# One step list for attention and router: 213 of 471 steps elsewhere, 20 entries of the engine tables changed

## The chip, the cores and the metric

The kernel runs on one core of a Trainium2 chip. Engines: TensorE for matmuls (PE; its weight loads are shown as PEld), VectorE (DVE), ScalarE (ACT), GpSimd (POOL) and SyncE (SP), which issues nearly all transfers (DMAs). The metric is the device time of one execution in microseconds. Three runs of the kernel before took 601.49, 602.51 and 603.44 us; the median is 602.51 us. A further execution was profiled: 600.41 us, of which 598.3 us lie between its first and its last instruction (the span). Times inside a trace are counted from the start of the span.

## The reference, cut to what matters

Three blocks follow one another on 2 x 768 tokens of 512 numbers:

```python
# attention, 2 batches x 8 heads x 768 x 64: local window of 16, plus one key and value per block of 32
k_sum = k.reshape(B, H, nb, 32, D).max(axis=3); v_sum = v.reshape(B, H, nb, 32, D).mean(axis=3)
a = softmax(concat([masked scores q.k, scores q.k_sum + log 32]))
x = a @ concat([v, v_sum])                      # then heads side by side: 1536 x 512
# router and experts: each token to the expert with the largest logit
logits = x/|x| @ (emb/|emb|).T / tau;  expert = argmax(logits);  gate = softmax(logits)[expert]
y[mask] = gate * (relu(x[mask] @ w1[e]) @ w2[e])    # 8 experts, 512 -> 1024 -> 512
# rational feed-forward, 512 -> 2048 -> 512
h = y @ w_in;  g = P(h) / (Q(h) + 1e-6);  out = g @ w_out
```

All is in float32; the large matrices go through the matmul engine as a high and a low part (whi and wlo, xhi and xlo).

## The kernel before, in words

The change touches the first part alone: attention, the router and the start of the experts. After it come 17 expert slots of 128 tokens (gemm1 at L967, gemm2 at L998) and the feed-forward (L946 to L948 and L1327), both unchanged.

Every engine runs its own instructions in the order in which the program emits them; there is no scheduler behind it (`manual_schedule`). SP's transfers are such a queue too. So the order in which Python calls the functions below is the order on each engine.

Attention works on 8 head pairs (n = 0 to 7; 0 to 3 are batch 0) and on 24 groups (g) of four blocks of 64 queries. Groups 0 to 2 read pair 0, 3 to 5 pair 1, 6 to 11 pairs 2 and 3, 12 and 13 pair 4, 14 and 15 pair 5, 16 to 19 pairs 6 and 7, 20 to 23 pairs 4 to 7. Tokens come in 12 chunks (c) of 128 for the router, which takes them two by two (k = 0 to 5). I name the steps by the letters that the new list uses:

- L n loads k, q and v of a pair (L147 to L158), W n the two halves of its windowed values vp (L160). Pair 0 and most of pair 1 are loaded ahead. The buffers of q and k are three, those of bd, kw and vw five.
- K n (prep_k, L171) builds the block-diagonal queries bd in two halves, the block maxima ks, their broadcast copy into kw, and the window copy into kw (I write bd5, ks7, kwb7 for the broadcast, kw7 for the window). The table BDE names the engines of the halves, KE that of the window copy: A is ACT, D is DVE, P is POOL.
- V n (prep_v, L199) sums values by blocks, on DVE or as a tree of six adds on POOL (VE). P n (prep2, L214) transposes the sums on PE and copies them to vw on ACT.
- S g scores on PE (L266), N g row minima on DVE (L280), X g exponentials on ACT (L288), T g transposes on PE (L294) and a copy on ACT or DVE (AE), O g the product with the values (L316), E g three DVE operations that divide and write the chunk (L323, L325, L331).
- f c transposes a chunk on PE (L390) and copies it (XE), q c its squares (QE; on POOL a tree of ten), Z c the logits (L423), m c maximum and its place on DVE, w c writes the chunk to memory; h, d, u, p k make the one-hot (L448), the ranks on PE (L498 to L505), the running sum (L453) and the two one-hot matrices (L522, L524). I 0 to I 4 set the router up, I 5 to I 7 load the first expert weights (w1(0), w2(0), w1(1)).
- The end: n0 to n2 norms, PC counts, tb the table of slots on DVE, F1 to F5 the tokens of the slots, g0 and g1 gathers on POOL, x0 the first slot's transposes, i and j the high parts of the first weights on ACT, l the low parts (wlo, L691), z0, z1, rc, rg the gates, k and y matmuls that only keep PE busy.

In the kernel before, the order comes from two places. For groups 0 to 22 a loop (L636) emits S g, T g-2, E g-4, N g, X g, O g-3, and then what the tables GK, GV, G2, GL, GR, GW, FO, FX and FQ put at that group, each function as a whole. From E19 on, the string DRAIN (L65) lists the steps one by one, and a step of several operations is advanced by one each time that it is named.

The scores' buffers in PSUM are two (ps_s), so S g needs N g-2 done; the transposes' buffer is one (ps_t), so a T needs the copy of the T before.

## Time and profile before

| | |
|---|---|
| runs | 601.49, 602.51, 603.44 us |
| profiled execution | 600.41 us, span 598.3 us |
| mean clock of PE | 0.986 of 2.4 GHz |
| PE busy | 573.0 us (96% of the span) |
| DVE busy | 471.4 us (79%) |
| ACT busy | 418.6 us (70%) |
| POOL busy | 264.0 us (44%) |
| first S | 6.62 us |
| first gemm1 matmul (L967) | 101.79 us |
| DMA share in the first ten of 40 slices, in tenths | 8 9 9 9 8 1 3 6 6 8 |

A slice is 15 us. The first seven slices are attention and router; in them the digits of PE are 4 8 9 8 9 9 9 and those of DVE 5 9 9 9 8 8 9. The waits name who released an engine that sat idle; an engine can be the limit of one stage and be idle in the next, so the shares over the whole span say little of these seven slices.

### The profile page before, as it was taken

The page shows a single profiled execution, that of the slowest core. Times are in us where ns is not written, and L with a number is a line of the kernel's source. Part 1 is how long each engine was busy: PE and PEld are TensorE (multiplying, and loading weights), DVE is VectorE, ACT ScalarE, POOL GpSimd, SP SyncE. Part 2 cuts the span into 40 slices and gives each one's busy share as a digit, 9 for nine tenths or more (in the row PEclk, how much of TensorE's full clock was granted, in tenths as well). Part 3 has the DMA queues.
Part 4 walks back from the last instruction along what each step waited for, and adds up shares of the span by engine and source line. Part 5 has one row for each costly group of instructions (what it writes and reads, how often), then busy time and mean ns, then how long its engine had stood idle before and what let it go on. Part 6 is the DMA issues. An engine that isn't in the chain of part 4 may idle for free. (4 is left out here: it accounts for less than half of the span.)

```text
span 598.3 us, 10282 instructions
## 1 busy us (share of the span) xinstructions
PE 573.0 (96%) x3137; PEld 468.3 (78%) x3137; DVE 471.4 (79%) x1025; ACT 418.6 (70%) x716; POOL 264.0 (44%) x281
## 2 busy tenths in 40 slices
PE   4898999999999999999999999999999999999994
PEld 3787885788888888888887888888888888888883
DVE  5999888978844896769777888888997777778874
ACT  5998845774536564566866998777778887766762
POOL 6478161158333550634032664414445763423424
PEclk9998997999999999999999999999999999999998
DMA  8999813668669996789974323110324200100101
GB/s 296 322 308 304 336 71 108 199 242 280 215 230 294 379 317 194 253 313 341 354 249 132 118 73 122 54 53 1 109 86 158 71 1 1 53 19 0 54 18 70
DMA packets 38749, 101.65 MB, mean 170 GB/s; under 512 B 6105, under 2 KB 6233, under 8 KB 38690
## 3 DMA queue, kind: packets, MB, share of 16 engines
q1 hardware_dynamic: 36210, 92.81, 46.1%
q0 software_dynamic: 2480, 8.15, 4.3%
q8 instruction: 25, 0.41, 0.3%
q14 instruction: 34, 0.28, 0.1%
HBM read 119.51 MB, written 19.18 MB: 232 GB/s over the span
## 5 line engine op out<-in xcount | busy, mean ns | idle before, releaser
L926 POOL TENSOR_SCALAR el<-el 128x512 f32<-128x512 f32 x32 | 66.9, 2098 | 95.0 <-ACT el L921 94.9
L691 DVE TENSOR_TENSOR wlo<-rw,whi 128x1024 fp32r<-128x1024 f32 x64 | 77.6, 1272 | 0.9 <-ACT whi L688 0.4
L1127 POOL TENSOR_TENSOR wlo<-el,whi 128x512 fp32r<-128x512 f32 (+1 forms) x33 | 42.2, 1278 | 77.2 <-ACT whi L1126 37.3
L688 ACT ACTIVATE whi<-rw 128x1024 fp32r<-128x1024 f32 x64 | 63.9, 1053 | 9.2 <-DMA rw<-w 3.7
L998 PE MATMUL py<-whi,hhi 128*128 128x512 f32 x136 | 53.9, 404 | 0.2 <-ACT hhi L985 0.2
L998 PE MATMUL py<-whi,hlo 128*128 128x512 f32 x136 | 52.7, 396 | 0.0
L967 PE MATMUL ph<-whi,xhi 128*128 128x512 f32 x128 | 49.8, 407 | 0.3 <-ACT xhi L681 0.3
L967 PE MATMUL ph<-whi,xlo 128*128 128x512 f32 x128 | 48.7, 397 | 0.0
L986 DVE TENSOR_TENSOR hlo<-pht,hhi 128x512 fp32r<-128x512 f32 x34 | 21.8, 682 | 27.9 <-ACT hhi L985 27.8
L1113 ACT ACTIVATE el<-el 128x512 f32<-128x512 f32 (+1 forms) x49 | 30.6, 624 | 14.9 <-DVE el L1107 14.8
L1327 PE MATMUL acc<-whi 128*128 128x512 f32 x130 | 39.1, 394 | 0.7 <-ACT whi L1126 0.7
L1105 ACT ACTIVATE el<-hg,ab 128x512 f32<-128x512 f32 (+1 forms) x33 | 22.4, 680 | 24.4 <-PE hg L948 24.3
L946 PE MATMUL hg<-x2h,whi 128*128 128x512 f32 (+1 forms) x100 | 39.5, 395 | 0.0
L947 PE MATMUL hg<-x2h,wlo 128*128 128x512 f32 (+1 forms) x100 | 39.2, 392 | 0.0
L948 PE MATMUL hg<-x2l,whi 128*128 128x512 f32 (+1 forms) x100 | 39.1, 391 | 0.0
L1327 PE MATMUL acc<-whi,wlo 128*128 128x512 f32 x130 | 38.7, 391 | 0.4 <-POOL wlo L1127 0.4
L1327 PE MATMUL acc<-wlo,whi 128*128 128x512 f32 x130 | 38.5, 390 | 0.0
L1119 DVE SCALAR_TENSOR_TENSOR el<-el,ab,hg 128x512 f32<-128x512 f32 (+1 forms) x33 | 24.3, 738 | 16.0 <-ACT hg L1115 15.2
L1127 POOL TENSOR_TENSOR xlo<-el,xhi 128x512 fp32r<-128x512 f32 (+1 forms) x16 | 20.2, 1262 | 37.6 <-issue 21.1
L1107 DVE SCALAR_TENSOR_TENSOR el<-el,ab,hg 128x512 f32<-128x512 f32 (+1 forms) x33 | 24.4, 738 | 15.4 <-ACT el L1106 15.2
L1114 ACT ACTIVATE el<-el,ab 128x512 f32<-128x512 f32 (+1 forms) x49 | 35.1, 717 | 1.6
L998 PE MATMUL py<-wlo,hhi 128*128 128x512 f32 x136 | 34.4, 395 | 0.0
(584 smaller groups left out, 1615.4 us busy)
## 6 DMA issues: line engine op xcount, KB each, us to landing
...
```

The costliest lines, as they stand in the source:

```text
L688: nc.scalar.activation(out=whi[:, i], in_=rw[s % 2, i // 4][:, i % 4], func=AF.Copy)
L691: eng.tensor_tensor(out=wlo[:, i], in0=rw[s % 2, i // 4][:, i % 4], in1=whi[:, i].bitcast(F32), op=ALU.subtract)
L926: eng.tensor_scalar(out=z, in0=z, scalar1=CLO, scalar2=CHI, op0=ALU.max, op1=ALU.min)
L946: nc.tensor.matmul(out=o, lhsT=lh, rhs=rh, start=start, stop=False)
L947: nc.tensor.matmul(out=o, lhsT=ll, rhs=rh, start=False, stop=False)
L948: nc.tensor.matmul(out=o, lhsT=lh, rhs=rl, start=False, stop=stop)
L967: nc.tensor.matmul(out=ph[n], lhsT=l[:, k], rhs=w, start=(k == 0 and not rl and l is hi), stop=(k == 3 and rl))
L998: nc.tensor.matmul(out=py, lhsT=l[:, f], rhs=w, start=(f == 0 and not rl and l is hi), stop=(f == 7 and rl))
L1113: nc.scalar.activation(out=a, in_=a, func=AF.Abs)
L1114: nc.scalar.activation(out=r, in_=a, func=AF.Ln, bias=ab[:, 7:8])
L1127: nc.gpsimd.tensor_tensor(out=lo, in0=g, in1=hi.bitcast(F32), op=ALU.subtract)
L1327: nc.tensor.matmul(out=acc[q], lhsT=l[:, q * P - o:(q + 1) * P - o], rhs=r, start=start, stop=stop)
```

## The change

The loop, its tables and DRAIN go; one string SCHED lists all 471 steps, and the generators get more yields, so that K, L, W can be taken apart too. Both lists hold the same steps; in the longest common order stand 258, the other 213 are at another place. Twenty entries of the tables BDE, VE, KE, QE, AE, XE and SE name another engine.

```diff
--- before.py
+++ after.py
@@ -41,31 +41,32 @@
 NTOK = B * S
 NT = NTOK // P
 E = 8
-BDE = {0: 'AA', 1: 'PD', 2: 'AA', 3: 'PD', 4: 'DA', 5: 'PD', 6: 'DP', 7: 'AA'}
-VE = {0: 'D', 1: 'P', 2: 'P', 3: 'D', 4: 'P', 5: 'P', 6: 'P', 7: 'P'}
-GK = {1: 1, 2: 3, 3: 4, 4: 9, 5: 11, 6: 11, 7: 13}
-GV = {1: 3, 2: 4, 3: 6, 4: 10, 5: 11, 6: 12, 7: 13}
-G2 = {0: 1, 1: 3, 2: 6, 3: 7, 4: 11, 5: 13, 6: 15, 7: 17}
-GL = {2: 0, 3: 0, 4: 5, 5: 7, 6: 7, 7: 11}
-QE = "PDDDADADPPDA"
-GR = [1, 5, 5, 8, 9, 12, 20, 19]
-GW = {1: 1, 2: 1, 3: 6, 4: 3, 5: 9, 6: 17, 7: 18}
-AE = "DADAAAAAAAAADAAAAAAAADAD"
-XE = "DADAADADAAAA"
-KE = {0: 'A', 1: 'D', 2: 'D', 3: 'A', 4: 'A', 5: 'P', 6: 'A', 7: 'P'}
-FO = [10, 11, 13, 15, 16, 18, 20, 21, 22, 23]
-FX = [4, 11, 15, 20, 14, 19, 22, 21]
-FQ = [15, 16, 15, 22, 17, 18, 18, 18, 22]
+BDE = {0: 'AA', 1: 'PA', 2: 'AA', 3: 'PD', 4: 'DA', 5: 'PP', 6: 'DD', 7: 'AA'}
+VE = {0: 'D', 1: 'P', 2: 'P', 3: 'P', 4: 'P', 5: 'P', 6: 'P', 7: 'P'}
+QE = "APDPAPADPDPA"
+AE = "AADAAAAAAAAADAAAAAAAADAA"
+XE = "AADDAAAADAAA"
+KE = {0: 'D', 1: 'D', 2: 'D', 3: 'A', 4: 'P', 5: 'P', 6: 'A', 7: 'P'}
 STOP = False
-MICRO = True
-TRACE = []
-SE = "DDDD"
+SE = "DPDD"
 NX, NM = 22, 26
 TS, OS = (), (0, 2)
-DRAIN = ("E4 T2 h3 E4 S E4 w8 w9 O3 M O2 T1 Z8 O1 d3 X m8 E3 E3 m8 E3 f9 E2 E2 E2 T0 f10 Z9 E1 u3 p3 p3 p3 u3 u3 R0 "
-         "E1 m9 E1 p3 O0 m9 Z10 R1 E0 E0 h4 d4 E0 w10 w11 u4 m10 f11 p4 Z11 p4 m10 q10 q9 p4 C p4 q11 n0 n1 u4 m11 u4 n2 n2 "
-         "i0 m11 h5 d5 n2 p5 PC k2a tb p5 n2 tb p5 n2 p5 F1 tb F2 g0 i2 tb n2 tb F3 k4b i1 tb tb tb tb tb i3 tb K0 k3a tb tb "
-         "K1 k1a tb K2 k1b tb j0 j1 F4 F5 g1 tb x0 k2b z0 z1 rc l0 rg l1 l2 l3 ")
+SCHED = ("K0 K0 K0 K0 K0 K0 K0 K0 V0 L3 S0 N0 X0 L2 L2 P0 S1 N1 L2 L3 S2 K1 K1 K1 K1 X1 K1 W1 L3 W1 I0 N2 T0 S3 "
+         "X2 T1 V1 P1 N3 K2 K2 K2 K2 K2 X3 W4 O0 S4 E0 E0 N4 X4 K3 T2 V2 E0 S5 K3 K3 K3 W2 W2 L4 K3 T3 I1 O2 N5 "
+         "X5 L5 O1 E1 E1 E1 I2 W3 W3 S6 T4 O3 E2 W4 L4 L4 E2 E2 V3 P2 S7 O4 L5 L5 N6 X6 T5 E3 S8 N7 X7 E3 I3 T6 "
+         "E4 E4 E4 P3 N8 X8 E3 O5 W5 E5 E5 E5 S9 T7 N9 O6 X9 K4 K4 K4 K4 K4 L6 L6 E6 E6 V4 I4 T8 E6 K5 S10 N10 "
+         "X10 O7 f0 S11 P4 T9 E7 E7 E7 N11 X11 L7 L6 L7 L7 w1 O8 K5 K5 Z0 K5 K5 E8 f1 K6 K6 m0 w0 V5 S12 N12 O9 "
+         "T10 K6 K7 E8 Z1 S13 m1 K7 m1 V6 T11 m0 h0 I5 E8 K6 E9 X12 E9 E9 K6 O10 P5 N13 X13 K7 S14 f2 N14 X14 T12 "
+         "O11 d0 S15 p0 E10 V7 K7 K7 E10 E10 f3 w2 u0 u0 u0 Z2 m2 m2 N15 T13 O12 E12 W6 X15 q2 P6 E11 S17 E12 E12 "
+         "q1 E11 E11 W5 S16 N16 p0 p0 Z3 T14 p0 f4 X16 O13 E13 E13 T15 N17 O14 m3 m3 w4 P7 S18 T16 w5 Z4 h1 E14 "
+         "E14 W6 E14 N18 X18 W7 q4 O15 E13 E15 E15 I7 f5 W7 m4 S19 T18 X17 m4 E15 q5 d1 p1 O16 N19 E16 u1 S20 T17 "
+         "u1 u1 X19 p1 p1 Z5 N20 E16 E16 O17 f6 E17 X20 m5 m5 h2 I6 E17 E17 S21 N21 p1 T19 q3 X21 S22 O18 Z6 q7 "
+         "m6 d2 f7 w7 p2 u2 u2 T20 E18 E18 E18 u2 N22 O19 q6 p2 f8 p2 p2 Z7 m7 q0 m7 q8 m6 h3 w3 w6 T21 S23 N23 "
+         "E19 E19 E19 q9 O20 X22 T22 Z8 O22 X23 O21 E20 E20 m8 m8 f9 E21 E21 E21 d3 p3 T23 Z9 E20 u3 f10 E22 E22 "
+         "p3 u3 p3 p3 E22 O23 Z10 w8 m9 m9 E23 E23 h4 u3 E23 w11 d4 w10 u4 f11 m10 m10 p4 p4 q10 Z11 C w9 p4 p4 "
+         "q11 n0 n1 u4 m11 m11 h5 d5 k2a n2 n2 n2 n2 p5 i0 p5 n2 p5 p5 PC tb tb n2 F1 tb tb j1 j0 F2 g0 u4 k4b tb "
+         "tb tb tb tb tb tb y0 tb tb tb tb i2 k3a i1 F3 y1 k1a i3 y2 k1b F4 F5 tb g1 x0 l0 l1 z0 z1 rc rg l2 l3 "
+         "k2b ")
 NEG = 1.0e30
 RS = 1536
 NA = E * RS // P
@@ -148,6 +149,7 @@
         b, hp = slots[n]
         q_t, k_t = qks[n % 3][:, 0:S], qks[n % 3][:, S:QK]
         nc.sync.dma_start(out=k_t, in_=I["kT"][b, hp, :, 0:SP])
+        yield
         nc.sync.dma_start(out=q_t, in_=I["qT"][b, hp])
         raw[n] = (q_t, k_t)
 
@@ -161,6 +163,8 @@
         b, hp = slots[n]
         i = n % NS
         for c in range(2):
+            if c:
+                yield
             j = slice(c * NJ // 2, (c + 1) * NJ // 2)
             nc.sync.dma_start(out=vw[i][LOC:LOC + WLP, j].rearrange("p j d -> p (j d)"),
                               in_=I["vp"][b, hp, c, :, 0:NJ * DV])
@@ -183,11 +187,14 @@
                 else:
                     nc.gpsimd.tensor_tensor(out=bd[i][s, j0:j1, s], in0=src,
                                             in1=eighth[s].unsqueeze(2).to_broadcast([64, NJ, QB]), op=ALU.mult)
+                yield
             if j0 == 0:
                 ks = wk.tile([P, NB], F32, name="ks")
                 nc.vector.tensor_reduce(out=ks, in_=k_t[:, WIN - 1:WIN - 1 + S].rearrange("p (n r) -> p n r", r=32),
                                         axis=AX.X, op=ALU.max)
+                yield
                 nc.vector.tensor_copy(out=kw[i][:, :, 0:NB], in_=ks.unsqueeze(1).to_broadcast([P, NJ, NB]))
+                yield
             if KE[n] == "D":
                 nc.vector.tensor_copy(out=kw[i][:, j0:j1, LOC:KW], in_=win(k_t, j0, j1))
             elif KE[n] == "A":
@@ -195,6 +202,7 @@
             else:
                 nc.gpsimd.tensor_tensor(out=kw[i][:, j0:j1, LOC:KW], in0=win(k_t, j0, j1),
                                         in1=one.unsqueeze(2).to_broadcast([P, j1 - j0, WL]), op=ALU.mult)
+            yield
 
     def prep_v(n):
         v_t = raw.pop(n)[2]
@@ -226,13 +234,16 @@
     ab = const.tile([P, 8], F32, name="ab")
     vcs = {}
     zero(0, nc.vector)
-    load_qk(0)
+    for _ in load_qk(0):
+        pass
     mask = cload("mask", [P, 3, KW])
     load_v(0)
     cst = cload("cst", [P, NCST])
     ident = cst[:, 0:P]
-    load_qk(1)
-    load_w(0)
+    for _ in load_qk(1):
+        pass
+    for _ in load_w(0):
+        pass
     load_v(1)
     nc.sync.dma_start(out=emb, in_=I["emb"])
     nc.sync.dma_start(out=tau, in_=I["tau"].to_broadcast([E, 1]))
@@ -566,21 +577,9 @@
     def keep_pace(src):
         nc.tensor.matmul(out=env["warm"][0:1, 0, 0:E], lhsT=src[:, 0:1], rhs=src[:, 0:E], start=True, stop=True)
 
-    prep_k(0)
-    prep_v(0)
-    LT, LO, LE = 2, 3, 4
-    sched = {}
     bts = {}
     xTs = {}
     zs_ = {}
-
-    def at(g, fn, *args):
-        sched.setdefault(g, []).append((fn, args))
-
-    def f1_(c, q=True):
-        xTs[c] = router_a(c)
-        if q:
-            router_q(c)
 
     def fz_(c):
         zs_[c] = router_z(c, xTs.pop(c))
@@ -592,55 +591,13 @@
                 bts[i] = dict(c0=2 * i, n=2, **{x: b6[x][:, 2 * i:2 * i + 2] for x in ("z", "m8", "i8")})
         return router_m(c, zs_.pop(c), bts[k])
 
-    def f2_(k, c):
-        fz_(c)
-        lace(fm_(k, c))
+    def fa_(c):
+        xTs[c] = router_a(c)
 
     def loads(n):
-        load_qk(n)
+        yield from load_qk(n)
+        yield
         load_v(n)
-
-    for n in range(8):
-        if n:
-            at(GK[n], prep_k, n)
-            at(GV[n], prep_v, n)
-        at(G2[n], prep2, n)
-    for n, g in GW.items():
-        at(g, load_w, n)
-    for n, g in GL.items():
-        at(g, loads, n)
-    for g, fn in zip(GR, (router_init0, router_init1, router_init4, router_init3, router_init2,
-                          lambda: wload(0, 0), lambda: wload(0, 1), lambda: wload(1, 0))):
-        at(g, fn)
-    batches = {0: (0, 1), 1: (2, 3), 2: (4, 5), 3: (6, 7), 4: (8, 9), 5: (10, 11)}
-    first = dict(enumerate(FO))
-    for c in first:
-        if c < 8:
-            at((max(FX[c], first[c]), 0), xw, c)
-        if c < 9:
-            at((first[c], 0), f1_, c, False)
-            at((max(FQ[c], first[c]), 0), router_q, c)
-    for k in range(4):
-        cs = batches[k]
-        for c in cs:
-            at(first[c] + 1, f2_, k, c)
-        l = first[cs[-1]]
-        for d, fn in ((2, router_h), (3, router_d), (3, router_u), (4, router_p)):
-            if k < 3:
-                at(l + d, lambda fn, k: lace(*filter(None, (fn(bts[k]),))), fn, k)
-
-    def run(g):
-        for fn, args in sched.pop(g, ()):
-            fn(*args)
-
-    for g in range(NG - 1):
-        s_mm(g)
-        t_mm(g - LT) if g >= LT else None
-        lace(o_ev(g - LE)) if g >= LE else None
-        s_sm(g)
-        o_mm(g - LO) if g >= LO else None
-        run((g, 0))
-        run(g)
 
     idx = const.tile([P, MAXS], U32, name="idx")
     xg = {}
@@ -808,68 +765,39 @@
         nc.tensor.matmul(out=pi[:, 0:MAXS], lhsT=env["mT"], rhs=sel, start=True, stop=True)
         nc.vector.tensor_scalar(out=idx[:, 1:MAXS], in0=pi[:, 1:MAXS], scalar1=float(NTOK), scalar2=None, op0=ALU.add)
 
-    G = NG - 1
-    ops = {"S": lambda: s_mm(G), "M": lambda: s_min(G), "X": lambda: s_exp(G), "C": close_att, "PC": count,
-           "tb": table, "F1": slot0_mm, "F2": slot0_ix, "F3": slots_mm, "F4": slots_ix, "F5": slots_id, "g0": lambda: gather(0), "g1": lambda: gather(1),
-           "x0": lambda: xtr(0), "gw": gw,
-           "R0": lambda: run(G), "R1": lambda: run(G + 1),
+    ops = {"C": close_att, "PC": count, "tb": table, "F1": slot0_mm, "F2": slot0_ix, "F3": slots_mm, "F4": slots_ix,
+           "F5": slots_id, "g0": lambda: gather(0), "g1": lambda: gather(1), "x0": lambda: xtr(0),
            "z0": lambda: router_z0(bts[6]), "z1": lambda: router_z1(bts[6]),
            "n0": lambda: router_n0(bts[6]), "n1": lambda: router_n1(bts[6]), "n2": lambda: router_n2(bts[6]),
            "rc": lambda: router_c(bts[6]), "rg": lambda: router_g(bts[6])}
-    for k in range(3):
-        ops[f"T{k}"] = lambda k=k: t_mm(G - k)
-    for k in range(4):
-        ops[f"O{k}"] = lambda k=k: o_mm(G - k)
-        ops[f"i{k}"] = lambda k=k: shi(0, k)
-        ops[f"l{k}"] = lambda k=k: slo(0, k, nc.gpsimd if SE[k] == "P" else nc.vector)
-    for t in DRAIN.split():
+
+    def family(name, keys, fn):
+        for k in keys:
+            ops[f"{name}{k}"] = lambda k=k: fn(k)
+
+    for name, fn in (("S", s_mm), ("N", s_min), ("X", s_exp), ("T", t_mm), ("O", o_mm), ("E", o_ev)):
+        family(name, range(NG), fn)
+    for name, fn in (("K", prep_k), ("V", prep_v), ("P", prep2), ("W", load_w), ("L", loads)):
+        family(name, range(len(slots)), fn)
+    for name, fn in (("f", fa_), ("q", router_q), ("w", xw), ("Z", fz_), ("m", lambda c: fm_(c // 2, c))):
+        family(name, range(NT), fn)
+    for name, fn in (("h", router_h), ("d", router_d), ("u", router_u), ("p", router_p)):
+        family(name, range(6), lambda k, fn=fn: fn(bts[k]))
+    family("I", range(8), lambda k: (router_init0, router_init1, router_init4, router_init3, router_init2,
+                                     lambda: wload(0, 0), lambda: wload(0, 1), lambda: wload(1, 0))[k]())
+    family("i", range(4), lambda k: shi(0, k))
+    family("j", range(4), lambda k: shi(0, 4 + k))
+    family("l", range(4), lambda k: slo(0, k, nc.gpsimd if SE[k] == "P" else nc.vector))
+    family("y", range(3), lambda k: keep_pace(env[("cs", "ge", "pr")[k]]))
+    started = {}
+    for t in SCHED.split():
         if t[0] == "k":
-            ops[t] = lambda n=int(t[1]): keep_busy(n)
-    for k, name in enumerate(("cs", "ge", "pr")):
-        ops[f"K{k}"] = lambda name=name: keep_pace(env[name])
-    for k in range(4):
-        ops[f"j{k}"] = lambda k=k: shi(0, 4 + k)
-    for k in range(5):
-        ops[f"E{k}"] = lambda k=k: o_ev(G - k)
-    for c in range(8, 12):
-        ops[f"Z{c}"] = lambda c=c: fz_(c)
-        ops[f"m{c}"] = lambda c=c: fm_(c // 2, c)
-        ops[f"w{c}"] = lambda c=c: xw(c)
-        if c > 8:
-            ops[f"f{c}"] = lambda c=c: f1_(c, False)
-            ops[f"q{c}"] = lambda c=c: router_q(c)
-    for k in range(3, 6):
-        ops[f"h{k}"] = lambda k=k: router_h(bts[k])
-        ops[f"d{k}"] = lambda k=k: router_d(bts[k])
-        ops[f"u{k}"] = lambda k=k: router_u(bts[k])
-        ops[f"p{k}"] = lambda k=k: router_p(bts[k])
-    started = {}
-    TRACE.clear()
-
-    def step(t):
+            keep_busy(int(t[1]))
+            continue
         if t not in started:
             started[t] = ops[t]()
-        g = started[t]
-        if g is None:
-            TRACE.append(t)
-            return False
-        r = next(g, 0)
-        if r is None or t not in done_:
-            TRACE.append(t)
-        if r is not None:
-            done_.add(t)
-        return r is None
-
-    done_ = set()
-    for grp in DRAIN.split():
-        ts = grp.split("+")
-        if MICRO:
-            for t in ts:
-                step(t)
-        else:
-            while ts:
-                ts = [t for t in ts if step(t)]
-    assert not sched, sched
+        if started[t] is not None:
+            next(started[t], None)
     tab_.close()
     rt_.close()
 
```

## Rows read from the trace of the kernel before

**Rows 1.** Windows by stage: start:end length, busy per engine (instructions), clock, DMA share, GB/s
```profile
20.00:50.00 30.00, 26.40 (x334) 23.09 (x329) 28.81 (x146) 29.30 (x66) 17.63 (x23) 1.00 1.03 317
58.00:80.00 22.00, 22.00 (x269) 20.01 (x267) 18.81 (x124) 16.79 (x49) 5.95 (x11) 1.00 0.73 267
80.00:102.00 22.00, 19.63 (x182) 13.60 (x177) 17.98 (x115) 11.65 (x24) 8.32 (x20) 0.84 0.30 97
102.00:116.00 14.00, 13.24 (x61) 10.03 (x61) 13.80 (x19) 8.46 (x12) 2.21 (x2) 1.00 0.53 140
```

**Rows 2.** Waits of PE, 5 to 105 us: total us, times, longest
```profile
PE pz L503 <- DVE oh L448: 2.0, 1, 2.0
```

**Rows 3.** Timeline of DVE, 47.5 to 51.5 us: start, duration, instruction
```profile
47.86 0.94 DVE L188 TENSOR_REDUCE ks<-rw 128x24 f32<-128x768 f32 x1
48.84 1.12 DVE L190 COPY kw<-ks 128x288 f32<-128x288 f32 x1
49.87 0.97 DVE L448 TENSOR_TENSOR oh<-cst,i 128x16 bf16<-128x16 f32 x1
50.77 0.68 DVE L299 COPY aT<-pt 118x512 f32<-118x512 f32 x1
```

**Rows 4.** Windows around the stretches in which PE's clock was low
```profile
48.60:52.00 3.40, 1.40 (x17) 1.30 (x14) 3.30 (x7) 2.32 (x3) 3.19 (x4) 0.99 0.97 382
52.00:55.40 3.40, 3.40 (x28) 3.06 (x28) 3.26 (x24) 2.09 (x7) 3.06 (x7) 0.51 0.78 194
89.50:96.30 6.80, 6.80 (x45) 4.55 (x46) 4.65 (x36) 3.17 (x7) 0.00 (x0) 0.50 0.56 171
```

**Rows 5.** Timeline 32 to 38 us: idle time ahead and releaser in brackets
```profile
32.22 1.06 POOL L207 TENSOR_TENSOR vs<-el 128x384 f32<-128x384 f32 x1 [10.23 <-DMA el<-vT]
...
33.86 0.54 DVE L182 TENSOR_SCALAR el<-rw 64x768 f32<-64x768 f32 x1
...
36.26 1.46 POOL L184 TENSOR_TENSOR bd<-qk,eighth 64x768 f32<-64x768 f32 x1 [0.96 <-DMA qk<-qT]
```

**Rows 6.** Durations by source line: ns min/median/max, first and last start
```profile
L190 DVE COPY kw<-ks x6: 311/542/1116, 4.9 to 48.8; 128x288 f32<-128x288 f32 x6
L448 DVE TENSOR_TENSOR oh<-cst,i x6: 145/174/967, 49.9 to 92.0; 128x16 bf16<-128x16 f32 x6
L417 DVE CUSTOM_DVE_ANT_0 junk<-xall x6: 669/684/785, 55.6 to 88.8; 128x512 bf16<-128x512 f32 x6
L691 DVE TENSOR_TENSOR wlo<-rw,whi x64: 1162/1219/1648, 103.1 to 317.3; 128x1024 fp32r<-128x1024 f32 x64
L926 POOL TENSOR_SCALAR el<-el x32: 1906/1920/2898, 127.7 to 439.6; 128x512 f32<-128x512 f32 x32
```

**Rows 7.** Timeline 40 to 57 us: values of pair 6, kw7, exponentials, group 16
```profile
44.97 1.00 POOL L207 TENSOR_TENSOR vs<-rw 128x384 f32<-128x384 f32 x1
...
47.72 2.07 POOL L196 TENSOR_TENSOR kw<-rw,one 128x1128 f32<-128x1128 f32 x1
...
52.41 1.24 ACT L288 ACTIVATE at<-sm,nm 128x118 f32<-128x118 f32 x4 [1.48 <-DVE nm L280]
...
56.13 1.05 PE L266 MATMUL sp<-kw,bd 128*128 128x118 f32 x8
```

**Rows 8.** The page's costliest groups: POOL's splits
```profile
L1127 POOL TENSOR_TENSOR wlo<-el,whi 128x512 fp32r<-128x512 f32 (+1 forms) x33 | 42.2, 1278 | 77.2 <-ACT whi L1126 37.3
```

**Rows 9.** Timeline of ACT in the opening
```profile
14.41 0.20 ACT L355 ACTIVATE ab<-ab 128x2 f32<-128x2 f32 x1 [0.78 <-DMA ab<-ab]
```

**Rows 10.** Timeline of the tail: group 23, the first expert's matmuls
```profile
78.64 1.05 PE L266 MATMUL sp<-kw,bd 128*128 128x118 f32 x8
...
80.83 0.27 DVE L280 CUSTOM_DVE_ANT_0 sm<-sp,mask 128x118 f32<-128x118 f32 x1
...
101.79 2.13 PE L967 MATMUL ph<-whi,xhi 128*128 128x512 f32 x8 [0.25 <-ACT xhi L681]
...
108.39 0.73 PE L967 MATMUL ph<-wlo,xhi 128*128 128x512 f32 x2 [0.40 <-DVE wlo L691]
```

## The prediction

> **What bounds the kernel now.** I first read the windows of the span by stage [rows 1]. From 116 us on the matmul engine (PE) is busy in every slice of the page and the chain that ended last runs through it up to the drain at the end, so this change can only move the moment at which that stretch begins, plus what it leaves behind on VectorE (DVE) up to 116 us. In 20 to 50 us ScalarE (ACT, 29.30 of 30.00) and DVE (28.81) are both full and PE is not (26.40); in 58 to 80 us PE is full (22.00 of 22.00) and the others are not; in 80 to 102 us no engine is full and PE's clock is down (0.84); in 102 to 116 us DVE is full again (13.80 of 14.00). So four stages, each with its own limit, and an edit is priced in the stage where it lands.
>
> Then the waits of PE up to 105 us [rows 2]: the longest behind the start and the opening is 2.0 us, the rank matmul of the first pair of chunks (d0) waiting for the one-hot that DVE makes (h0). The timeline of DVE there [rows 3] shows why: the broadcast copy of ks7 takes 1.12 us and h0 0.97 us, both far above their usual size, while GpSimd (POOL) runs its own copies. The windows by clock [rows 4] show what followed: PE, idle for most of 48.6 to 52.0, got 0.51 of its clock (1.2 of 2.4 GHz) in 52.0 to 55.4; the same happened in 89.5 to 96.3.
>
> Last I read the transfers. SyncE (SP) issues the loads in order and they land in order; the reader that waits shows when: v of pair 4 releases POOL at 32.22, q of pair 5 at 36.26 [rows 5]. In the old list v4 is the 15th transfer behind v1 and q5 the 19th, hence 4.04 us for 4 places, 1.01 us a place.
>
> **The change part by part.** Counted step by step, 258 of the 471 steps keep their order among each other, 213 stand elsewhere, none is added or dropped. The tables put 20 entries on another engine; what that does to the sums of 0 to 116 us:
> - DVE loses bd1 and bd5 halves and takes one of bd6 (net one of 0.54 [rows 5]); it loses the sum of v3 (about 0.95, the size of the ks reduction beside it [rows 3]), three squares net (0.68 each [rows 6]), three transposed copies net (about 0.68, [rows 3] has one), one wlo split (1.22 [rows 6]); it takes kw0 (estimate 0.7, under the 0.94 of the reduction over the same tile). Sum: -0.54 - 0.95 - 2.04 - 2.04 - 1.22 + 0.7 = -6.1 us.
> - ACT stays within 1 us: it loses two window copies and gains copies and one square.
> - POOL gains the sum of v3 (2.75) and kw4 (2.07; both [rows 7]), two squares net (trees of ten small adds each) and wlo1. Its splits in the trace are half as wide and take 1.28 [rows 8], so 2.56 us.
>
> The opening gains nothing: kw0 on DVE lets the first scores start some tenths earlier, but ACT then waits for the small ab load in any case, until 14.41 [rows 9], and that load keeps its place.
>
> The loads. K, Q and V of pair 4 go behind the second halves of the vp tiles: q4 from place 14 to 17, so at 36.26 - 2 x 1.01 = 34.2 us, v4 from 15 to 18 (35.2), q5 stays at 19. DVE took q4 at 33.86 without a wait [rows 5]; now it waits about 0.35 us, and group 10 starts no earlier than before. What was gained ahead of it is lost here. The vp halves of pairs 5 to 7 now queue on SP behind chunk writes 4 and 5, which wait for E11; readers of W7 come four groups later, so I price this at nothing; without that cover it would be two places, 2 us.
>
> POOL's chain then runs from v4: V4 2.75 (from 44.97 to 47.72 in [rows 7]), two bd5 halves at 1.46, kw5 2.07, V5, V6, V7 2.75 each, and only then kw7 2.07: 35.2 + 2.75 + 2.92 + 2.07 + 8.25 + 2.07 = 53.3 us. Groups 16 and 17 need kw7; group 16 started at 56.13 [rows 7]. So POOL allows 2.8 us at most there.
>
> The stall at 48.6: h0 is now issued before group 13, so PE's 2.0 us wait goes and, with it, the reason for the slow clock after it. What is late next? ACT had 1.48 us of idle ahead of group 14's exponentials [rows 7]; gone, ACT allows 1.5 to 2. DVE has the same operations between the row minima of groups 13 and 15 in either list (kwb7, the copies and E10 are only shuffled past group 14), so it wins only what the two stretched operations cost, 0.81 and 0.80 (against 0.31 and 0.17 for the same lines in [rows 6]), less the 0.35 of q4: 1.2 us. The least of the three is DVE's, and I take **1.2 us** at group 16 (bounds: -4 if kw7 is late, rival A; +2.8).
>
> From 58 to 80 us PE is the limit and its work is the same, so the 1.2 us are carried, and DVE's lighter load (the squares, the copies) is hidden behind PE; if PE were not full, it would be worth up to 4 us.
>
> The tail. Group 23's minima started at 80.83 [rows 10], 2.2 us behind its first matmul, because E19 and a copy stood ahead on DVE; now E19 stands behind it. But PE puts Z8, two O and f9 between, so only part of that reaches the last chunk. And PE was busy all of 89.5 to 96.3 at half clock [rows 4], so whatever of it is not waiting could be half as long. Between 0 and 2.2, I take **0.6 us**, nearer to the end at which PE's order decides.
>
> The wlo1 split on POOL takes 1.22 us from the full DVE between 102 and 108 us; PE waited 0.40 us for the last of these splits at 108.39 [rows 10]. Between -1.3 (DVE held up for POOL's 2.56 in place of its own 1.22) and +1.2, I take **0.6 us**, nearer to the wait that PE shows.
>
> Do moved operations slow DVE? Here a row speaks: wlo on DVE takes 1.16 to 1.65 us and POOL's clip 1.91 to 2.90 [rows 6], the long ones where both run. That is about 0.4 us on DVE and 1.0 on POOL for a meeting, not the whole length of the other's instruction; it is why I leave the sums above as they are. The Trainium skill (SBUF — State Buffer, section "SBUF: two separate sides") says more: GpSimd and DVE share a port pair as an exclusive lock for the whole instruction and "the other fully blocks", for DVE operations with two SBUF inputs too. By that rule the moved wlo1 relieves nobody (rival D); the 1.65 against 1.22 agrees with a loss, not with its size.
>
> Sum: 1.2 + 0.6 + 0.6 = **2.4 us**. The profiled execution took 600.41 us (span 598.3), hence 598.0; the median of the runs shown is 602.51, 2.1 above it, hence **600.1 us**.
>
> **The rivals.**
> - A, POOL becomes the bound (slower). Place: kw7, last in POOL's chain from v4. Price: if each of the eight operations of 1 us and more in it meets DVE and takes 0.9 us longer (the 2.90 against 1.91 of [rows 6]), kw7 ends at 60.5 us; groups 16 and 17 then start 4.4 us later than in [rows 7], less 0.9 for Z2 that is already done, plus 1.7 for a slow clock behind the gap, less 1.2 of tail and wlo1: +4.0, 606.5 us. It decides from a kw7 later than about 57.3. For it: pair 4's v comes later and V3, kw4, a bd5 half stand ahead. Against it: the rows of V6 and kw7 were taken beside a full DVE and are not stretched.
> - B, the gain does not reach PE. DVE is as full between groups 13 and 15 as before and the stretched operations are stretched again, now beside kw7 at another place; only part of the tail and of wlo1 is left: -1.0, 601.5 us. For it: 28.81 of 30.00 on DVE; against it: the stall of d0 is surely gone.
> - D, wlo1 holds DVE up. POOL's 2.56 us stand in the way of the splits of rows 0, 2 and 3 on DVE, so the last one, and PE behind it, is 1.3 us later instead of 0.6 earlier: 1.2 + 0.6 - 1.3 = 0.5, hence 602.0 us. For it: the stretched rows of [rows 6]; against it: they are stretched by a third, not by the other's length. This is where the rule of the Trainium skill above would lead.
> - C, all three allowances come: 2.8 us at group 16, no slow clock before 96 us (1.5), 1.1 for wlo1: -5.4, 597.1 us. For it: PE idles 3.6 us in 20 to 50 and 2.4 in 80 to 102 [rows 1]; against it: three engines must each have slack at once.
>
> **How the numbers follow.** Forecast 0.38 (its own range 599.0 to 601.2), C 0.20, B 0.21, D 0.06, A 0.15. What can be told from no change here is 0.3%, 1.8 us: faster is below 600.7, slower above 604.3. Of the forecast's 0.38 some 0.33 lies below 600.7, with C 0.53; B, D and the rest of the forecast 0.32; A 0.15. For 8 in 10 the range goes down to 596.8, just past C, and up to 604.0, which leaves out most of A.
>
> **What would show it.** Right: PE's wait for h0 is gone and no clock below 1.0 in 50 to 56 us; DVE waits for q4 near 34 us; kw7 on POOL ends near 53 us and groups 16 and 17 start about 55; the first expert matmul (L967) starts near 100, not 101.79. Wrong: PE waiting for kw7 past 57 us (A), DVE full and ACT waiting for it near 52 us again (B), DVE's last wlo split of the first expert later than before (D), a first expert matmul before 97.5 (C), or a new slow-clock window at another place, which none of my steps has.

## The result: slower by 0.7%, and where the time went

| | before | changed |
|---|---|---|
| median of 20 runs | 603.67 us (601.48 to 608.59) | 607.64 us (605.95 to 611.62) |
| ratio | 1 | 1.0066, 95% interval 1.0046 to 1.0086 |
| profiled execution | 600.41 us, span 598.3 | 610.07 us, span 608.0 |
| row minima of groups 8, 12, 23 | 30.17, 44.57, 80.83 us | 33.34, 47.86, 83.03 us |
| first expert matmul | 101.79 us | 106.09 us |
| its second half starts behind it by | 7.17 us | 8.65 us |

I had forecast 600.1 us and "faster". The change costs 4.0 us between the medians. The profiled pair lies 9.7 us apart, since the one execution was a fast one of its kernel and the other a slow one; what follows takes places from the pair, prices from the ratios, and asks executions of other kernels that run the same list in a stretch whether a place of the pair holds.

The stages of the changed kernel (columns as in [rows 1]), and its three stretches of low clock behind 30 us:

```profile
20.00:50.00 30.00, 24.73 (x288) 21.96 (x286) 27.21 (x124) 23.94 (x56) 19.69 (x26) 0.94 1.02 289
58.00:80.00 22.00, 22.00 (x278) 20.24 (x278) 17.96 (x127) 18.09 (x49) 14.25 (x36) 1.00 0.82 266
80.00:102.00 22.00, 19.49 (x182) 14.09 (x180) 19.14 (x113) 13.08 (x32) 10.93 (x25) 0.77 0.41 126
102.00:116.00 14.00, 11.57 (x62) 7.68 (x61) 12.96 (x30) 6.73 (x10) 4.35 (x4) 1.00 0.18 38
...
33.60:37.00 3.40, 3.40 (x28) 3.26 (x28) 2.04 (x15) 1.35 (x5) 0.00 (x0) 0.50 1.05 359
50.70:54.10 3.40, 3.32 (x27) 3.20 (x28) 2.75 (x14) 3.39 (x8) 2.93 (x7) 0.50 1.01 375
91.60:101.90 10.30, 9.16 (x50) 4.84 (x50) 8.14 (x55) 6.67 (x13) 1.64 (x5) 0.50 0.55 182
```

In 20 to 50 us, where ACT and DVE were both full before, no engine is full now, and PE does less (24.73 against 26.40). Up to 125 us the mean clock is 0.92; in the profile of before it is 0.95. The waits of PE (total, times, longest) say what it stood for:

```profile
PE o L327 <- DVE xall L342: 3.8, 2, 2.0
...
PE pz L509 <- ACT zs L448: 1.2, 1, 1.2
...
PE ph L895 <- DVE xlo L639: 1.0, 1, 1.0
```

The wait for h0 [rows 2] is gone, as forecast; four others stand in its place, three of them here and one, for the gates of the third slot (1.5 us at 143 us), below. One cause shows when DVE's timeline is laid beside POOL's (start, duration, instruction):

```profile
29.76 0.13 DVE L381 RECIPROCAL tau<-tau 8x1 f32<-8x1 f32 x1
29.87 1.71 DVE L382 TENSOR_TENSOR esq<-esq 8x1 f32<-8x1 f32 x1
...
33.34 0.27 DVE L291 CUSTOM_DVE_ANT_0 sm<-sp,mask 128x118 f32<-128x118 f32 x1
...
44.02 3.63 DVE L186 TENSOR_SCALAR bd<-rw 64x768 f32<-64x768 f32 x2
...
87.86 0.51 DVE L526 TENSOR_SCALAR ps<-ps 128x2 f32<-128x2 f32 x1
...
105.51 2.75 DVE L720 TENSOR_TENSOR tb<-tb,cst 128x38 f32<-128x38 f32 x1
...
108.50 0.68 DVE L639 TENSOR_TENSOR xlo<-pht,xhi 128x512 fp32r<-128x512 f32 x1
```

```profile
29.50 2.07 POOL L203 TENSOR_TENSOR el<-rw,one 128x1128 f32<-128x1128 f32 x1 [2.71 <-DMA rw<-kT]
...
43.84 2.12 POOL L203 TENSOR_TENSOR kw<-qk,one 128x1128 f32<-128x1128 f32 x1
45.92 1.32 POOL L215 TENSOR_TENSOR vs<-v 128x384 f32<-128x384 f32 x1
...
87.74 0.61 POOL L415 TENSOR_TENSOR sq<-xall 128x256 f32<-128x256 f32 x1 [0.73 <-DVE rd L334]
...
105.77 2.43 POOL L648 TENSOR_TENSOR wlo<-rw,whi 128x1024 fp32r<-128x1024 f32 x1
```

L382 multiplies eight numbers and takes 1.71 us (0.15 in e2, where kw4 is not on POOL); it ends at 31.58, and POOL's kw4 at 31.57. The last addition on the slots' table (L720) ends at 108.26, POOL's wlo1 at 108.20. The halves of bd6 (L186, 0.54 each as a rule) end 0.4 us behind the instruction that they met: the second at 47.65, POOL's addition (L215) at 47.24. L720 starts 0.26 us ahead of wlo1, while POOL is still in a gather; in the profile of before the same addition beside the same gather took 0.20 us, so it was wlo1 that held it. These are two lines of before, DVE and POOL:

```profile
101.54 0.20 DVE L763 TENSOR_TENSOR tb<-tb,cst 128x38 f32<-128x38 f32 x1
...
100.81 0.99 POOL L650 DMA_INDIRECT xg<-xs,idx  x1 [3.06 <-DVE idx L809]
```

Up to 125 us I count 12 held operations in the changed kernel, 10.1 us above their usual sizes, and 7 before, 3.2 us. The rows ahead of the prediction hold two of the seven: the copy of ks7 ends at 49.96 [rows 3], 0.17 behind kw7 on POOL [rows 7], and h0 at 50.84, 0.03 behind this instruction of POOL in the profile of before:

```profile
49.75 1.06 POOL L207 TENSOR_TENSOR vs<-el 128x384 f32<-128x384 f32 x1
```

### The profile page after: what moved, and what is told of

Same layout as the page of the kernel before. It is cut to its first block, busy times and chain, and to the rows that moved or that the text cites. A ratio compares the mean times of both kernels' runs of the same rounds, so it can differ in the third digit from the quotient of the medians.

```text
span 608.0 us, 10300 instructions
## 1 busy us (share of the span) xinstructions
PE 575.8 (95%) x3137; PEld 468.9 (77%) x3137; DVE 474.9 (78%) x1015; ACT 419.9 (69%) x719; POOL 278.6 (46%) x310
## 5 line engine op out<-in xcount | busy, mean ns | idle before, releaser
L854 POOL TENSOR_SCALAR el<-el 128x512 f32<-128x512 f32 x32 | 65.6, 2059 | 97.9 <-ACT el L849 97.8
L648 DVE TENSOR_TENSOR wlo<-rw,whi 128x1024 fp32r<-128x1024 f32 x63 | 76.3, 1270 | 0.7 <-ACT whi L645 0.4
L914 DVE TENSOR_TENSOR hlo<-pht,hhi 128x512 fp32r<-128x512 f32 x34 | 21.8, 682 | 28.5 <-ACT hhi L913 18.3
```

The costliest lines, as they stand in the source:

```text
L648: eng.tensor_tensor(out=wlo[:, i], in0=rw[s % 2, i // 4][:, i % 4], in1=whi[:, i].bitcast(F32), op=ALU.subtract)
L854: eng.tensor_scalar(out=z, in0=z, scalar1=CLO, scalar2=CHI, op0=ALU.max, op1=ALU.min)
```

## The experiments

In the table T is the start of the first expert matmul, "tail" the time from the row minima of group 23 to T, "half" the time from T to the second half, "gates" PE's wait for the gates of the third slot; these four and the row minima of group 12 come from one execution each, the ratio from all.

| kernel | ratio to before (95%) | group 12 | T | tail | half | gates |
|---|---|---|---|---|---|---|
| before | 1 | 44.57 | 101.79 | 20.96 | 7.17 | none |
| changed | 1.0066 (1.0046 to 1.0086) | 47.86 | 106.09 | 23.06 | 8.65 | 1.5 |
| e1 wlo1 on DVE | 1.0025 (0.9999 to 1.0051) | 45.86 | 104.70 | 22.71 | 7.36 | 1.8 |
| e2 kw4 on ACT | 1.0035 (1.0009 to 1.0062) | 47.34 | 105.15 | 23.13 | 8.56 | 1.5 |
| e3 bd6 on ACT | 1.0039 (1.0008 to 1.0070) | 43.41 | 102.27 | 22.99 | 8.70 | 1.5 |
| e4 these three | 1.0035 (1.0006 to 1.0065) | 44.33 | 103.23 | 23.01 | 7.37 | 1.5 |
| e5 and gates first | 0.9989 (0.9958 to 1.0019) | 45.99 | 105.10 | 23.16 | 7.00 | none |
| e6 and q10 on ACT | 0.9963 (0.9932 to 0.9993) | 44.17 | 100.86 | 20.80 | 7.00 | 1.3 |
| e7 new list, old tables | 1.0079 (1.0050 to 1.0108) | 46.71 | 106.20 | 24.33 | 7.37 | 2.3 |
| e8 old list, new tables | 1.0073 (1.0040 to 1.0105) | 48.24 | 104.39 | 20.62 | 8.63 | 1.5 |
| t1 before, wlo1 on POOL | 1.0047 (1.0018 to 1.0075) | 45.41 | 102.36 | 20.75 | 8.44 | 0.8 |
| t2 the same in quarters | 1.0022 (0.9996 to 1.0049) | 51.76 | 107.09 | 21.02 | 7.51 | 0.6 |
| t3 kw4 with one source | 1.0090 (1.0055 to 1.0125) | 48.24 | 106.54 | 23.11 | 8.62 | 1.6 |
| t4 tail only | 1.0011 (0.9982 to 1.0040) | 47.86 | 104.93 | 20.92 | 7.01 | none |
| u1 tail, POOL in pieces | 0.9997 (0.9961 to 1.0034) | 45.07 | 105.19 | 20.75 | 7.01 | 1.3 |
| u2 e6, POOL in pieces | 0.9986 (0.9951 to 1.0020) | 46.03 | 104.13 | 21.78 | 7.00 | none |

One execution has to be read beside others that run the same instructions. Up to 95 us before, t1 and t2 run the same ones, and their group 12 starts at 44.57, 45.41 and 51.76. Changed, e1 and t4 share their attention, and there it starts at 47.86, 45.86 and 47.86. So it is not shown that the 3.3 us by which the pair differs at group 12 come from the change. The tail is another matter: 20.8 to 21.0 us in before, t1 and t2, 22.7 to 23.2 in the seven kernels with the new list and the squares of chunk 10 on POOL (changed, e1 to e5, t3), 20.8 to 21.8 in the four with these squares on ACT (e6, t4, u1, u2). In the changed kernel tail, half and gates together are 5.1 us over before (2.1, 1.5 and 1.5), more than the 4.0 between the medians.

**Taking the meetings out of the changed kernel.**

```diff
-SE = "DPDD"
+SE = "DDDD"                       # e1
-KE = {... 4: 'P', ...}
+KE = {... 4: 'A', ...}            # e2
-BDE = {... 6: 'DD', ...}
+BDE = {... 6: 'AA', ...}          # e3; e4 is all three
```

> The changed kernel with the one split wlo1 back on DVE; its profile showed a small DVE addition on the table (L720) stand for 2.75 us until POOL's wlo1 ended, beside 0.20 us before. Theory L (a DVE operation from SBUF to SBUF that starts while POOL is in an instruction stands until that instruction ends): L720 is back to 0.2 us, the matmuls of the first expert's second half start about 7.2 us behind its first one (8.65 in the changed kernel, 7.17 before), and the wait of 1.5 us for the gathered gates of the second slot goes: 1.5 to 3 us faster than the changed kernel (607.6), so 604.6 to 606.1, ratio to the kernel before 1.002 to 1.004. Theory O (what was lost lies in the moved order and PE's clock in the attention): DVE has 1.2 us more to do, time 607 to 609, ratio 1.006 or more.

> The changed kernel with the window copy of pair 4 (kw4) on ACT again instead of POOL. Theory L: the multiplication of eight numbers on DVE at L382 takes 0.15 us instead of 1.71, group 8's row minima start 1.6 us earlier, PE's wait of 1.8 us for the divides of group 3 shrinks below 0.5 and the slow clock behind it goes; part of it is taken back at bd6, which still meets POOL: 0.5 to 3 us faster than 607.6, about 605.6, ratio 1.003. Theory O: L382 is short, but the divide of group 3 still stands behind I3 and group 8 in the list, so PE's wait stays over 1 us, and the end moves by less than 0.5 us: 607 to 608.

> The changed kernel with both halves of bd6 on ACT instead of DVE, where they took 2.35 and 1.27 us (0.54 is the usual size). Theory L: DVE gains 3.6 us between groups 11 and 12, group 12's minima start 2 to 3.5 us earlier than 47.86, and what is left at the end is 1 to 3 us: 604.6 to 606.6, ratio 1.0015 to 1.005. Theory O: group 12 comes earlier by the 1.1 us of work alone that DVE loses, PE then waits for the divides of group 8 in any case (2.04 us at 50.78), and the end moves by less than 0.7 us: 607 to 608.

> The three edits together: kw4 and bd6 on ACT, wlo1 on DVE. Theory L: the three large meetings of DVE and POOL are gone, the three gains add up to 4 to 8 us: 600 to 603.5, ratio 0.994 to 1.000. Theory O: only work has moved between engines, the list is the same: 606.5 to 608.5, ratio 1.005 or more.

Theory L had the places right. In e1 the second half starts 7.36 us behind the first matmul, but the gates' wait, which L wanted gone, is 1.8; in e2 L382 takes 0.15 us, group 8 starts at 30.59 instead of 33.34, and PE's wait for the divides of group 3 is 0.24 us instead of 1.80, against theory O; in e3 group 12 starts 4.45 us earlier, though e1, with the changed kernel's attention, has it 2.0 earlier too. The times say less: the intervals of e1 to e4 all overlap that of the changed kernel. And the gains don't add up: e4 stays at 1.0035, where L wanted 1.000 or less. Its trace still shows the gates' wait of 1.5 us, and p3 on DVE held at 85 to 87 us by POOL's squares of chunk 10. In e2 the 2.75 us won at group 8 are down to 0.52 at group 12, for DVE then waits for the queries of pair 4 (q4), which the new list loads later:

```profile
35.90 0.55 DVE L186 TENSOR_SCALAR el<-rw 64x768 f32<-64x768 f32 x1 [2.37 <-DMA rw<-qT]
```

```diff
-... g1 x0 l0 l1 z0 z1 rc rg l2 l3
+... g1 x0 z0 z1 rc l0 rg l1 l2 l3     # e5: e4 and this
-QE = "APDPAPADPDPA"
+QE = "APDPAPADPDAA"                   # e6: e5 and this
```

> The kernel with all three edits, and at the end of the list the four steps of the gates back in the place that they had before: z0 z1 rc before the first split (x0 z0 z1 rc l0 rg l1 l2 l3 instead of x0 l0 l1 z0 z1 rc rg l2 l3). Theory G (the rest of the loss is a second chain: gates written late, gathers of the later slots late, POOL's first clip late, DVE's xlo of the third slot behind it, PE waiting 1.5 us near 139 us): the write of the gates lands about 6.6 us behind the first expert matmul instead of 7.9, PE's wait for gts is below 0.3, and the time is 1 to 1.5 us under the three edits: 604.5 in the chips' mean, ratio 1.000 to 1.002. Theory N (that wait has another cause, the slower transfers behind the gathers): it stays above 1 us, ratio 1.003 to 1.004.

> The same, and the squares of chunk 10 on ACT instead of POOL; there their first three instructions (0.6 to 0.7 us each) held the four operations of p3 on DVE for 0.51, 0.53, 0.84 and 0.59 us instead of 0.16, 0.15, 0.27 and 0.32. Theory L (a DVE operation from SBUF to SBUF stands until POOL's instruction ends): p3 takes its usual 1.0 us instead of 2.5, m9 comes 1.5 us earlier, PE's wait of 1.2 us for d4 shrinks below 0.4 and PE's slow stretch in the tail is 6.8 us instead of 10.2; the first expert matmul comes 1.5 to 3 us earlier than in the three edits (103.2), and the time is 1 to 2.5 us under the kernel with the gates first: ratio 0.996 to 1.000. Theory O (the order of the tail itself is worse): p3 is shorter but the chain of chunks 9 to 11 keeps its length, below 0.5 us.

e6 came in theory L's range. e5, at 0.9989, lies a little under theory G's 1.000, with no wait for the gates, as G said. e6 is faster than the kernel before, by an interval that ends at 0.9993; from e5 to e6 one letter takes the tail from 23.16 to 20.80 us. In e6's trace p3 takes its usual sizes and the first expert matmul starts at 100.86:

```profile
84.89 0.14 DVE L526 TENSOR_SCALAR ps<-ps 128x2 f32<-128x2 f32 x1
...
85.07 0.16 DVE L528 SCALAR_TENSOR_TENSOR ps<-ps 128x2 f32<-128x2 f32 x1
...
85.26 0.29 DVE L533 TENSOR_SCALAR ohb<-cst,ps 128x128 f16<-128x128 f32 x1
```

Only the gates' wait came back there (1.3 us), though the gates are written 3.1 us behind T in both kernels. POOL waited longer for the gathers to land, first in e5, then in e6:

```profile
121.37 0.22 POOL L1073 COPY gts<-xg 128x1 f32<-128x1 f32 x1 [7.30 <-DMA xg<-xs,idx]
130.05 0.97 POOL L1073 COPY gts<-xg 128x1 f32<-128x1 f32 x1 [5.26 <-DMA xg<-xs,idx]
...
117.89 0.63 POOL L1073 COPY gts<-xg 128x1 f32<-128x1 f32 x1 [8.09 <-DMA xg<-xs,idx]
127.22 0.73 POOL L1073 COPY gts<-xg 128x1 f32<-128x1 f32 x1 [6.19 <-DMA xg<-xs,idx]
```

So the place of the gates is not all of that wait: theory N's slower gathers are a part of it, and why they take longer in one execution no run tells.

**List and tables apart.** e7 has the changed list with the twenty old entries; in e8 SCHED spells out the old order, step by step, and the twenty entries are new.

> The new list with all twenty table entries as they were before. Theory L: most meetings go (kw4 on ACT, wlo1, v3, three squares and the rest on DVE), bd6 keeps one locked half, and DVE has 6 us more work; gates still late: ratio 1.001 to 1.004. Theory T (the loss is POOL's and DVE's load by the tables alone, the list is harmless or better): ratio 0.996 to 0.999, as I forecast for the list. Theory O (the list alone is what loses): ratio 1.006 or more.

> The old order, step by step, with the twenty new table entries. Theory L: wlo1 on POOL holds DVE at the table or at the splits for 1 to 2.4 us, kw4 and v3 on POOL meet other operations of DVE than in the new list, some of them locked: ratio 1.002 to 1.006. Theory T: the same as the changed kernel, 1.006. Theory O: as before or better, 0.997 to 1.001.

Each half alone is as slow as both together. By its ratio e7 is what theory O said and e8 what theory T said, and each of the two kernels refutes the other's theory: neither half is harmless beside the old other one. L's range was too low for e7 (1.004 at most) and, by the median, a little for e8, so the holds alone do not account for e7.

The places differ. e8 has the late half (8.63) and the gates' wait (1.5), but a tail of 20.62: in the old order the squares of chunk 10 on POOL held DVE for 0.7 us, in the changed kernel for 1.6. e7 has the half nearly as before (7.37) and the longest tail, 24.33: the new list puts the norms (n0, L469) ahead of the running sum of the fifth pair (u4, L464), and with the old tables n0 waits for squares on POOL, so PE waits 2.4 us for that sum. The gates add 2.3 us there, the divides 3.5. So list and tables belong to one another. From e7, DVE:

```profile
95.93 0.17 DVE L469 TENSOR_SCALAR rw__701<-ssq 128x12 f32<-128x12 f32 x1 [1.31 <-POOL ssq L422]
96.02 0.16 DVE L464 TENSOR_TENSOR roh<-roh,oh 128x8 bf16<-128x8 bf16 x1
```

**One POOL instruction by itself.** t1 is the kernel before, its list spelled out, with wlo1 on POOL; every other instruction of every engine is that of before, in the same order. In t2 that instruction is cut into four.

```diff
-SE = "DDDD"
+SE = "DPDD"                       # t1
-eng.tensor_tensor(out=wlo[:, i], ...)
+for a in (four slices of 256 columns):
+    eng.tensor_tensor(out=wlo[:, i, a], ...)      # t2, where eng is POOL
```

> The kernel before with one edit: the split wlo1 on POOL. Theory L (a DVE operation from SBUF to SBUF that meets a running POOL instruction stands until that ends): the table's last addition or the operation behind it on DVE stands for 1.5 to 2.5 us, and the matmuls of the first expert's second half start 8.2 to 8.7 us behind its first matmul instead of 7.2: ratio 1.001 to 1.004. My forecast's reading (a meeting costs DVE about 0.4 us, the full DVE is relieved of 1.2): they start 6.6 to 7.2 us behind it, ratio 0.998 to 1.000.

> The same, and POOL's wlo1 cut into four instructions of 256 columns. Theory L: a hold ends with the piece that is running, so no DVE operation stands longer than about 0.7 us more than its size, and the second half starts 7.0 to 7.9 us behind the first matmul: ratio 0.999 to 1.002. Theory B (the two engines share a bandwidth, and DVE loses time in proportion to POOL's work): as with one piece, about 2.4 us lost in all, 8.2 us or more.

t1, DVE and POOL:

```profile
101.97 2.75 DVE L720 TENSOR_TENSOR tb<-tb,cst 128x38 f32<-128x38 f32 x1
...
104.95 0.68 DVE L639 TENSOR_TENSOR xlo<-pht,xhi 128x512 fp32r<-128x512 f32 x1
```

```profile
102.22 2.42 POOL L648 TENSOR_TENSOR wlo<-rw,whi 128x1024 fp32r<-128x1024 f32 x1
```

t2, DVE and POOL:

```profile
106.71 0.43 DVE L720 TENSOR_TENSOR tb<-tb,cst 128x38 f32<-128x38 f32 x1
...
107.18 0.65 DVE L728 TENSOR_SCALAR rg<-tb 128x57 int32<-128x57 f32 x1
107.76 0.75 DVE L730 TENSOR_TENSOR rg<-tb 128x18 int32<-128x18 f32 x1
```

```profile
106.97 2.91 POOL L648 TENSOR_TENSOR wlo<-rw,whi 128x256 fp32r<-128x256 f32 x4
```

One edit of one letter makes the kernel before slower by 0.5%, through the hold that theory L gave and with the half at 8.44 us. In quarters no operation stands longer than 0.75 us and the half starts at 7.51: the hold is by instruction, not a share of a bandwidth. The time of t2 can be told neither from that of t1 nor from that of before. Up to 95 us t2 runs the same instructions as the kernel before, and still its group 12 started 7.2 us later. The copy of ks4, 0.31 us in the profile of before, stood there through the end of a half of bd5 and the whole of kw5 behind it, so a hold can run on over POOL's next instruction:

```profile
38.60 2.82 DVE L196 COPY el<-ks 128x288 f32<-128x288 f32 x1
```

```profile
37.76 1.46 POOL L188 TENSOR_TENSOR bd<-qk,eighth 64x768 f32<-64x768 f32 x1 [1.16 <-DMA qk<-qT]
39.19 2.06 POOL L203 TENSOR_TENSOR kw<-qk,one 128x1128 f32<-128x1128 f32 x1
```

So which meetings happen differs between executions of the same instructions; how much of the spread of the times comes from them is not shown.

**What kind of POOL instruction.**

```diff
-nc.gpsimd.tensor_tensor(out=kw..., in0=win(...), in1=one..., op=ALU.mult)
+nc.gpsimd.tensor_scalar(out=kw..., in0=win(...), scalar1=1.0, op0=ALU.mult)    # n == 4
```

> The changed kernel with POOL's window copy of pair 4 as a multiplication with a constant (one source) instead of one with a broadcast tile (two sources). By POOL's clip of one source, 1.92 us for 512 columns, it takes some 4.2 us, twice as long. Theory L1 (every POOL instruction holds DVE): L382 on DVE, 1.71 us in the changed kernel, stands for 3 to 4 us, group 8 comes 2 us later than 33.3: ratio 1.008 or more. Theory L2 (only POOL instructions of two sources hold DVE to their end; beside the clip of one source DVE's splits took 0.4 us more and no longer): L382 takes less than 0.6 us and group 8's minima start 1.2 us or more earlier, for all that POOL's instruction is longer: ratio 1.003 to 1.006.

```profile
29.45 0.13 DVE L381 RECIPROCAL tau<-tau 8x1 f32<-8x1 f32 x1
29.55 2.02 DVE L382 TENSOR_TENSOR esq<-esq 8x1 f32<-8x1 f32 x1
```

```profile
28.66 3.10 POOL L203 TENSOR_SCALAR el<-rw 128x1128 f32<-128x1128 f32 x1 [0.89 <-DMA rw<-kT]
```

L2 falls: one source holds DVE too, until 0.19 us before its end. It stood 2.0 us and not the 3 to 4 of L1, since POOL's instruction took 3.1 and not the 4.2 that I had worked out from the clip. The reciprocal of tau started inside the same POOL instruction and took its 0.13 us. The time (1.0090) can't be told from that of the changed kernel.

**The two halves of the loss, and pieces in place of moves.**

```diff
 # t4: the changed kernel with SE, QE and the gates of e1, e5 and e6; u1: t4 and this; u2: e6 and this
-nc.gpsimd.tensor_tensor(out=kw[i][:, j0:j1, ...], ...)
+four instructions of three blocks each, for n < 7; the first addition of V5 in two
```

> The changed kernel with the three edits of the tail alone: wlo1 on DVE, the gates first, the squares of chunk 10 on ACT; kw4 on POOL and bd6 on DVE stay as changed. Theory L: the attention is late as in the changed kernel (group 12's minima near 47.9, group 23's near 83), the tail behind group 23 is 3 us shorter, the first expert matmul starts at 103 to 104.5 instead of 106.1, PE waits less than 0.5 us for the gates: ratio 1.000 to 1.003. Theory O (the meetings of the attention decide alone, the tail was waiting for them): first expert matmul at 105 or later, ratio 1.004 or more.

> The kernel with the three edits of the tail, and no work moved in the attention: POOL's window copies of pairs 4 and 5 are cut into four instructions of three blocks each, and the first addition of V5 into two. Theory L (the attention's loss is DVE standing behind whole POOL instructions): DVE's small operation in I3 stands below 0.7 us instead of 1.7 to 2.1, the two halves of bd6 together below 2.4 instead of 3.6, group 12's minima start 1.5 to 3 us earlier than 47.9, the first expert matmul 1 to 3 us earlier than 104.9: ratio 0.996 to 0.999. Theory M (what helped in the kernels with kw4 and bd6 on ACT was that POOL and DVE had less to do): POOL has the same work and more instructions, group 12 stays near 47.9 or comes later, ratio 1.001 or more, as with the tail alone.

> The fastest kernel so far (kw4 and bd6 on ACT, wlo1 on DVE, gates first, squares of chunk 10 on ACT; ratio 0.9963) with the same cuts of kw5 and V5. Theory L: its large meetings are gone already, what is left of kw5 and V5 meets little on DVE: within 1 us of it, ratio 0.994 to 0.998. Theory M: four instructions cost POOL some 0.4 us more than one, and kw7 at the end of its chain moves by as much: ratio 0.997 to 1.000.

t4 stands at 1.0011 with the attention as late as in the changed kernel: of the way from 1.0066 to e6's 0.9963 the three edits of the tail gave 0.0055 and the attention 0.0048, each uncertain by some 0.004. So these three edits, wlo1, the gates and the squares, are enough to take the loss away; T came at 104.93, a little behind L's 104.5. In u1 the two DVE operations in I3 took 0.22 and 0.58 us, bd6 1.59 and group 12 started at 45.07, each as theory L had it and with no work moved. The time did not follow (0.9997, L wanted 0.999 or less): in that execution the running sum u0 met kw7, which was left whole, PE ran at half its clock from 58.9 to 65.7 us, and the first expert matmul started at 105.19. M is not excluded by the time, only by the rows: u1 could not be told from t4, nor u2 from e6.

## Why the prediction was wrong

The step that failed is the paragraph "Do moved operations slow DVE?". I priced a meeting at "about 0.4 us on DVE ... not the whole length of the other's instruction". The runs show the whole rest of POOL's instruction: 1.71 us instead of 0.15 for L382, 2.75 instead of 0.20 for L720. The row that I took the price from was DVE's split beside POOL's clip [rows 6], one kind of meeting and, as it came out, the one that is different; the two stretched rows at the stall [rows 3] I read as a mishap of that place and even booked their going as a gain, without asking which instruction of POOL they ended with. The rule that says this stood in my text: the Trainium skill (SBUF — State Buffer, section "SBUF: two separate sides") calls the port pair of GpSimd and DVE an exclusive lock for the whole instruction. The trace agrees: 2.75 us for L720 in the changed kernel and in t1 alike. It does not agree for the split beside the clip (last section). I applied the rule to one place and gave it 0.06. The change puts 13 us more on POOL up to 125 us (71.2 instead of 58.3), so a price for meetings had to be asked for at every part of it.

What this did to the sum: I had 0.6 us gained in the tail and 0.6 by wlo1, and nothing for the gates; the rows show 2.1, 1.5 and 1.5 us lost.

Step by step:
- Stages: right as to 58 to 80 us, where PE is full again. In 20 to 50 us "DVE is full" was a little misread, for an operation that is held counts as busy: of the 28.81 us about 1.2 were two held copies (41.21 and 48.84 us).
- Group 16: forecast 1.2 us earlier, 3.8 later in the pair (58.10 to 61.88). By the other executions that is open: t1 and t2 have it at 58.88 and 64.42, e1 and t4 at 60.45 and 62.48. The stall of d0 went; in the pair held operations took more than its place (1.56 us at L382, 2.5 at bd6), PE idled at other places, and its clock fell there (33.6 and 50.7 us). That a new slow stretch would come at another place I had named as what none of my steps had.
- The sums of work by engine could not show this: by my sum DVE lost 6 us of work, and in the pair it stood 6.9 us longer in meetings.
- Loads: V4 started at 37.61, not 35.2, and DVE, late itself, waited for no q4. It set nothing in this kernel: kw7 ended at 56.95 (forecast 53.3), and group 17 started at 59.20 without waiting for it. In e2, e4, e5 and e7 DVE did wait for q4, 0.9 to 2.4 us, until 35.9 to 37.6 instead of the 34.2 that I had, so the load was priced too low. Rival A, whose 606.5 us is near the measured time, was not what happened.
- Tail: forecast 0.6 us gained; from group 23's minima to the first expert matmul it took 23.1 us instead of 21.0. POOL's squares of chunk 10 held the operations of p3 for 1.6 us, and m9 and d4 came late behind them; with these squares on ACT the tail is 20.8 to 21.8.
- wlo1: forecast 0.6 gained, measured 1.5 lost (half at 8.65 against 7.17), of which 1.3 go in e1 with the split back on DVE. This is rival D, with the place and the price (1.3) as they were put, though the operation held was the table's addition and not a split.
- The gates: z0 z1 rc rg moved behind two splits, and I gave the move no price at all. In the changed kernel they are written 5.6 us behind the first expert matmul instead of 3.0, POOL's gathers follow, and then POOL's first clip; DVE's xlo of the third slot stands behind that in its queue. PE had no such wait in the profile of before, where the first clip started 25.9 us behind the first expert matmul instead of 29.7. Three lines of the changed kernel, and the clip of before:

```profile
115.12 1.57 POOL L607 DMA_INDIRECT xg<-xs,idx  x1 [6.92 <-DMA xs<-gat]
...
135.75 3.82 POOL L854 TENSOR_SCALAR el<-el 128x512 f32<-128x512 f32 x2
...
143.14 0.50 PE L895 MATMUL ph<-whi,xlo 128*128 128x512 f32 x1 [1.50 <-DVE gts L642]
...
127.70 4.78 POOL L926 TENSOR_SCALAR el<-el 128x512 f32<-128x512 f32 x2
```

- The base: the median of 602.51 stood on three runs; over 20 it is 603.67, and a single execution of this kernel can differ by 7 us.

What stays open: the rest of the 9.7 us of the profiled pair (4.3 to the first expert matmul, 1.5 at the half and 1.5 at the gates are placed, about 2.4 are spread over short waits behind them); whether the new attention by itself is later or earlier than the old; why the gathers took longer in e6; and what decides in which execution PE's clock falls.
